# Sparse attention and MLP in one kernel: ScalarE instead of GpSimd scales the words of the weights in the first slots, and the first unit of weights moves ahead in ScalarE's order

## The chip, the cores and the metric

The kernel runs on one core of a Trainium2 chip. A core has five engines with instruction streams of their own, which meet only at semaphores: TensorE (PE; its weight loads are listed as PEld), VectorE (DVE), ScalarE (ACT), GpSimd (POOL) and SyncE (SP), which here issues most of the transfers. The metric is the device time of one execution in microseconds (us), as the median of several runs. Before the change it is 1530.93 us.

## What is computed

The reference is top-k attention followed by an MLP with an exact GELU, all in float32:

```python
scores = scale * np.matmul(q, k.transpose(0, 1, 3, 2))      # 8 x 8 heads, 576 x 576, head_dim 64
kth = np.partition(scores, -32, axis=-1)[..., -32:-31]
scores = np.where(scores >= kth, scores, -1e9)
attn = np.exp(scores - scores.max(-1)) ; attn /= attn.sum(-1) + 1e-9
x = (attn @ v).transpose(0, 2, 1, 3).reshape(4608, 512)
h = x @ w_in                                                 # 512 x 2048
out = (0.5 * h * (1 + erf(h / sqrt(2)))) @ w_out             # 2048 x 512
```

## The kernel before, in words

The program is written with a manual schedule: each engine executes its instructions in the order in which the Python code emits them, and waits in that order.

**Items and slots.** Two heads make a pair, and 128 query rows of both heads of a pair make an item. A loop (`for n in range(ahead)`, L1086) emits one slot for each item. In slot n several items are under way at different stages: the scores of item n+2 (`scores`: PE's L339 for the last keys and L376 for the rest, brought out of PSUM by ACT's L347 and L384), the 32 largest values of item n on DVE (`top_k`: MAX8 in L471, MATCH_REPLACE8 in L474, with lists made by DVE's L412 and POOL's L437 and L445), the mask and exponential of item n-1 on ACT (`select`, L505, twice, and `softmax`, L517, twice, with the row sums `den`), the transposes of item n-2 (PE's L561 and L595 in the first slots, where the factor 1/den is put in by a diagonal matrix; L567 and L597 later; ACT's copies L577 and L602), and the product with v for item n-3 in every second slot (PE's L659, copied into xT by ACT's L664).

**What ties the engines together in a slot.** POOL first adds the unit of weights of this slot (L233), then does `smaller(n+1)` (L445), `add_small(n-1)` on den (L498), `threshold(n)` (L485 neg, L486 bias), `normalise(n-1)` (L531, the tile `diag`) and `sum_up(n+2)` (L437). DVE takes the reciprocal of den of item n-1 (L492) at the end of `top_k(n)`, so DVE waits there for POOL's L498, and that one for ACT's L517. PE's L561 waits for `diag`.

**The opening.** START is 10. In the slots 0 to 9 the MLP has not begun: PE fills up with matmuls on idle data (`keep_busy`, L1045, tile `warm`). The MLP's first matmul (L717, `h_ps`) comes in slot 10, as soon as xT is there. Afterwards pieces of the MLP are strewn over the slots. The pairs 0 to 3 are transposed by PE in the slots up to 3 (L287, tile `tp_qk`, copied by L292 into `kt` and `qm`); these pieces are kept in `prep_in`, and slot 0 has the keys of the third pair.

**The weights.** w_in and w_out come in as 16 units of 128x2x512 words, one for each of the slots 1 to 10 and 13 to 18. They are float64 in memory; a unit comes by two transfers on SP's queue, one for each 128 rows (`load_weights`, L190), into parts of w_out_sb and w_sum that aren't in use yet, and is turned into float32 by four instructions over its words: L207 on ACT (from the high words, into `below`), a scaling of the words `w` by 2**-13 as integers, L218 on ACT (`below` to the destination `d`), and L233 on POOL (d + w). The scaling does not depend on L207. It is done by DVE (L209) in the slots 13 to 18, by POOL (L213) in the slots 3, 5, 7 and 9 (`ON_POOL = range(3, START, 2)`), and by ACT (L217) in the rest. The first three belong to `weights_size`, which is called at the end of slot n for the unit of slot n+1 (L1188); the add stands first in slot n+1 (L1093). `load_weights(n+2)` stands behind it at the end of slot n, and a unit's buffer is the one of the unit two slots earlier, save for some that use w_sum, so its transfers wait for that unit's L233.

Of the kernel before, what the change touches and what calls it, by code (L numbers as in the profile page):

```python
# [14 lines left out]
def kernel(  # L15
# [19 lines left out]
    nc = tc.nc  # L35
    f32, i32, u32 = mybir.dt.float32, mybir.dt.int32, mybir.dt.uint32
    bf16, i16, u16 = mybir.dt.bfloat16, mybir.dt.int16, mybir.dt.uint16
    AF = mybir.ActivationFunctionType
    ALU = mybir.AluOpType
# [108 lines left out]
    START = 2 * NP + 2  # L148
    WARM = 9
    PAIRED = 0  # L150
    ON_DVE = range(START + 1, START + 9)
    ON_POOL = range(3, START, 2)
    DIAGS = START - 1
    SINGLE = range(18, 28)
    words = {}
# [7 lines left out]
    SLOT_OF = dict(zip(ORDER, [*range(1, START + 1), *range(START + 3, START + 9)]))  # L163
    UNIT_IN = {n: u for u, n in SLOT_OF.items()}
    unit_in = UNIT_IN.get
# [30 lines left out]
    def parts(u):  # L196

        t, dst = words[u], weights_of(u)[3].bitcast(i32)
        return t[:, :, 0::2], t.bitcast(mybir.dt.int16)[:, :, 2::4], t[:, :, 1::2], dst

    def weights_size(u):


        if u not in words:
            return
        w, first, below, d = parts(u)
        nc.scalar.activation(below, first, func=AF.Prelu, bias=high, scale=2.0**-40, alpha=2.0**40)  # L207
        if on_dve(u):
            nc.vector.tensor_scalar(  # L209
                w.bitcast(i32), w.bitcast(u32), 2.0**-13, None, op0=ALU.mult  # L210
            )
        elif SLOT_OF[u] in ON_POOL:
            nc.gpsimd.tensor_scalar(  # L213
                w.bitcast(i32), w.bitcast(u32), 2.0**-13, None, op0=ALU.mult
            )
        else:
            nc.scalar.activation(w.bitcast(i32), w.bitcast(u32), func=AF.Copy, scale=2.0**-13)  # L217
        nc.scalar.activation(d, below, func=AF.Prelu, bias=low, scale=2.0**59, alpha=2.0**-40)  # L218

    def on_dve(u):  # L220

        return SLOT_OF[u] in ON_DVE

    def waits(u):

        return u == ORDER[-1]
# [3 lines left out]
    def weights_add(u):  # L230
        if u in words:
            w, _, _, d = parts(u)
            nc.gpsimd.tensor_tensor(d, d, w.bitcast(i32), op=ALU.add)  # L233
        made.add(u)
# [129 lines left out]
    def scores(i, second=False):  # L364
        if i >= N or i in S_of:
            return
        pair, t = items[i]
        S_of[i] = s = work.tile([P, 2 * S], f32, tag="s", bufs=6, name="s")
        s_ps = pair_tile("s_ps", "l1" if second else "pr")
        if not few[0]:  # L370
            last_keys(i, bank("t_ps"))()
        if t < NM:
            q_t, kt = q_of[pair][:, t * P : (t + 1) * P], kt_of[pair]
            for e in range(2):
                rows = slice(e * D, (e + 1) * D)
                nc.tensor.matmul(  # L376
                    s_ps[:, e], lhsT=q_t[rows, :], rhs=kt[rows, 0:SM], start=True, stop=True
                )
            if i == 0:

                nc.scalar.activation(s[:, 0:SM], s_ps[:, 0], func=AF.Copy, scale=scale)
                nc.scalar.activation(s[:, S + TL :], s_ps[:, 1], func=AF.Copy, scale=scale)  # L382
                return
            nc.scalar.activation(spread(s, S + TL, SM), s_ps, func=AF.Copy, scale=scale)  # L384
        else:

            for r in range(2):
                kt = kt_of[pair + r]
                for e in range(2):
                    rows = slice(e * D, (e + 1) * D)  # L390
                    nc.tensor.matmul(  # L391
                        s_ps[half(r, e), r, :], lhsT=kt[rows, SM + P + e * TL : SM + P + (e + 1) * TL],
                        rhs=kt[rows, 0:SM], start=True, stop=True,
                    )
            s2 = s.rearrange("p (r n) -> p r n", r=2)
            nc.scalar.activation(s2[:, :, 0:SM], s_ps, func=AF.Copy, scale=scale)
# [12 lines left out]
    def larger(i):  # L409

        if paired(i):
            nc.vector.tensor_tensor(lists_of[i][:, :, 0], *halves_of(i), op=ALU.max)  # L412
# [87 lines left out]
    def select(i, e):  # L500

        if i < 0 or i >= N:
            return
        st, s = stat_of[i], row(i, e)
        nc.scalar.activation(s, s, func=AF.Prelu, bias=st["neg"][:, e : e + 1], scale=1.0, alpha=STEEP)  # L505
        selected.add((i, e))
# [113 lines left out]
    def closes(i):  # L620

        if not few[0] or i < 0 or i >= N:
            return False
        pair, t = items[i]
        return t < NM and t % 2 == 1 and pair % NP == NP - 1

    def copy_x():
        while copies:
            copies.pop()()
# [393 lines left out]
    def room_in(n):  # L1023

        x = n - START - 1
        if x < 1:
            return 4
        if x >= len(sizes):
            return 0
        return sizes[x] + (1 if x % 2 == 0 else -1)  # L1030
# [55 lines left out]
    for n in range(ahead):  # L1086

        left[0] = room_in(n)
        few[0] = n > START + 2
        eager[0] = n > N  # L1090
        left[0] += closes(n - 3) - closes(n - 2)
        if not waits(unit_in(n)):
            weights_add(unit_in(n))  # L1093
        if n > 0:
            larger(n + 1)
        for piece in squares_in.pop(n, []):
            piece()
        two = few[0] and n % 2 == 0 and n + 3 < N and items[n + 3][1] < NM
        scores(n + 2, two)
        if two:  # L1100
            scores(n + 3)
        product = attend(n - 3)
        late = n > START
        if n < START:

            for e in range(2):
                select(n - 1, e)
            softmax(n - 1, 0)
        copy_x()
        if n == START:  # L1110

            for e in range(2):
                select(n - 1, e)
            softmax(n - 1, 0)
        if waits(unit_in(n)):
            weights_size(unit_in(n))
            weights_add(unit_in(n))
        mlp(1)
        if closes(n - 3):
            ready[0] = n_tok[0]  # L1120
        if few[0] and n % 2:
            run_gelus()
        tr = transposes(n - 2)
        if product and n > START and done[0] < len(pieces) and pieces[done[0]][0] > ready[0]:

            for piece in tr[:1]:
                piece(n + 2 if few[0] else None)
            tr, ready[0] = tr[1:], n_tok[0]
        if not few[0] and n > START:
            softmax(n - 1, 0)  # L1130
        mlp(1)
        if not late:
            softmax(n - 1, 1)
        if few[0]:
            softmax(n - 1, 0)
            if n % 2:
                mlp(ODD)
        mlp(1)
        prep = prep_in.pop(n, [])
        if n == START + 1:  # L1140

            for piece in prep:
                piece(None)
            prep = []
        if len(prep) > 1 and len(tr) == 3:
            tr, prep = tr[:1] + prep[:1] + tr[1:], prep[1:]
        now = tr[:-1]
        if few[0]:
            now, tr, prep = tr + prep[:1], [], prep[1:]
        for x, piece in enumerate(now):  # L1150
            piece(n + 2 if few[0] else None)
            ready[0] = n_tok[0]
            if few[0] and x == 2:
                break
            mlp(1)
        ready[0] = n_tok[0]
        if late:
            softmax(n - 1, 1)
        if n > 0:
            smaller(n + 1)  # L1160
        add_small(n - 1)
        for piece in tr[-1:] + prep:
            piece(None)
            mlp(1)
        if n < START:

            keep_busy(4 if n == 0 else 8 if product else 20 if n == 1 else 14 if n < 5 else 18, ident)

        run_gelus()
        mlp(left[0])  # L1170
        run_gelus()
        if n < N:
            top_k(n, lambda: inverse(n - 1))
            if n == 0:
                larger(1)
        else:
            inverse(n - 1)
        threshold(n)
        if n == 0:
            smaller(1)  # L1180
        normalise(n - 1)
        sum_up(n + 2)
        if n in sums_in:
            weight_sums(sums_in[n])
        run_small(6)

        if not waits(unit_in(n + 1)):
            weights_size(unit_in(n + 1))  # L1188
        for m in (n + 1, n + 2):

            if m > 2 and waits(unit_in(m)) == (m == n + 1):
                load_weights(m)
        if n < NP:
            load("v", n)
        if n == 5:
            load("q", SQUARES)
            load("k", SQUARES)
# [38 lines left out]
```

## Time and profile before

| | |
|---|---|
| median of 3 runs | 1530.93 us (1529.75 to 1532.0) |
| the profiled execution | 1529.7 us, its span 1527.8 us |
| granted clock of TensorE, mean | 0.996 |
| PE busy | 1508.4 us (99%) |
| DVE busy | 1235.3 us (81%) |
| ACT busy | 1152.8 us (75%) |
| POOL busy | 1149.9 us (75%) |
| L213 on POOL | 4 instructions |
| L217 on ACT | 6 instructions |

A timeline row of the profile gives the start in us from the begin of the span, the duration, the engine, the line of the kernel, the operation, the tiles (out<-in), shapes and types and, in brackets, how long the engine was idle before and what ended that. Consecutive instructions of ACT overlap a little, so starts are subtracted from starts where the cost of one in its sequence is asked for. A row of a chain of waits gives the start and the length of the piece, with the engine and line that it is put down to. A row of the waits gives the engine and line that waited, for whom, the us in total, the number of times and the longest. A row of busy time by stretches gives the stretch and its length, then the busy us (with the number of instructions) of PE, PEld, DVE, ACT and POOL, the granted clock, the share of the transfers, and GB/s.

### The profile page before, as it was taken

The numbers are of one execution on the slowest core, as the hardware profiler recorded it, in microseconds if no ns is written. First come the engines' busy times: TensorE is split into PE (matmuls) and PEld (weight loads), VectorE is DVE, ScalarE is ACT, GpSimd is POOL, SyncE is SP. The second block draws the span as 40 slices with busy tenths as digits, with TensorE's granted clock in tenths as the row PEclk, the third lists the DMA queues.
The fourth block names the chain that finished last, engine by engine and source line by source line (L and its number), as shares of the span: only waits on it lengthen the run. The fifth ranks groups of instructions, "written<-read, shape, count | busy, mean of one in ns | idle before, by whom it ended". The sixth has DMA issues, their size and how long they took to land.

```text
span 1527.8 us, 26920 instructions
## 1 busy us (share of the span) xinstructions
PE 1508.4 (99%) x9233; PEld 1191.6 (78%) x9233; DVE 1235.3 (81%) x3270; ACT 1152.8 (75%) x2034; POOL 1149.9 (75%) x1295
## 2 busy tenths in 40 slices
PE   7999999999999999999999999999999999999999
PEld 5776677887777778888877778788787777888887
DVE  7889899988888878788888887888888887877701
ACT  6989977777877787877777777787777878787730
POOL 6997667867887868777797878786788786877742
PEclk9999999999999999999999999999999999999999
DMA  6424310021101110012201111011110111000000
GB/s 178 134 101 116 85 46 1 22 37 34 24 19 28 38 40 15 1 30 47 39 15 22 27 30 46 1 25 36 32 24 22 24 30 32 15 1 15 8 14 14
DMA packets 195016, 56.27 MB, mean 37 GB/s; under 512 B 185888, under 2 KB 186432, under 8 KB 194880
## 3 DMA queue, kind: packets, MB, share of 16 engines
q1 hardware_dynamic: 193616, 54.14, 15.1%
q8 instruction: 72, 1.18, 0.3%
q14 instruction: 64, 0.52, 0.1%
q10 hardware_dynamic: 1200, 0.39, 0.1%
q0 software_dynamic: 64, 0.03, 0.0%
HBM read 45.08 MB, written 9.44 MB: 36 GB/s over the span
## 4 chain that ended last, share of the span: by engine, by line
PE 93%; DVE 3%; POOL 2%; DMA 1%; SPq 0%; ACT 0%; issue 0%; DVEq 0%
PE h_ps L717 34%; PE y_ps L861 20%; PE o L659 9%; PE tp L597 8%; PE s_ps L376 7%; PE seven L859 3%; PE y_ps L823 2%; PE y_ps L805 2%; PE y_ps L826 2%; PE tp_t L339 2%; PE o L670 1%; PE s_ps L391 1%; PE tp_t L567 1%; DVE top L471 1%; DVE lists L474 1%; POOL w_out_sb L213 1%
## 5 line engine op out<-in xcount | busy, mean ns | idle before, releaser
L717 PE MATMUL h_ps<-xT,w_in_sb 128*128 128x256 f32 (+1 forms) x2560 | 544.0, 361 | 0.0
L717 PEld LDWEIGHTS h_ps<-xT,w_in_sb 128*128 128x128 f32 x2560 | 433.8, 191 | 70.8 <-issue 25.3
L471 DVE MAX8 top<-lists 128x8 f32<-128x576 f32 (+1 forms) x792 | 477.2, 642 | 0.1
L474 DVE MATCH_REPLACE8 lists<-top,lists 128x288 f32<-128x288 f32 (+1 forms) x528 | 307.4, 587 | 0.0
L540 POOL TENSOR_TENSOR s<-s,rden 128x1152 f32<-128x1152 f32 x135 | 285.4, 2114 | 0.3 <-DVE rden L492 0.3
L498 POOL TENSOR_SCALAR den<-den 128x2 f32<-128x2 f32 x144 | 31.7, 220 | 280.3 <-ACT s L517 278.4
L517 ACT ACTIVATE s<-s,bias 128x576 f32<-128x576 f32 x288 | 223.3, 776 | 11.6 <-issue 0.7
L505 ACT ACTIVATE s<-s,neg 128x576 f32<-128x576 f32 x288 | 224.6, 784 | 0.0
L611 ACT COPY pt<-tp 128x1024 f32<-128x1024 f32 x133 | 135.1, 1016 | 110.7 <-PE tp L597 110.7
L492 DVE RECIPROCAL rden<-den 128x2 f32<-128x2 f32 x144 | 23.7, 164 | 218.4 <-POOL den L498 218.1
L445 POOL TENSOR_TENSOR lists<-lists 128x576 int32<-128x576 int32 x132 | 186.3, 1412 | 4.0
L437 POOL TENSOR_TENSOR lists<-s 128x576 int32<-128x576 int32 x133 | 187.1, 1407 | 0.0
L659 PE MATMUL o<-pt,raw_v 128*64 128x256 f32 x1280 | 152.9, 384 | 0.7 <-ACT pt L602 0.4
L659 PEld LDWEIGHTS o<-pt,raw_v 128*64 128x64 f32 x1280 | 86.3, 136 | 85.9 <-issue 44.3
L861 PE MATMUL y_ps<-w_out_sb,sum 128*128 128x256 f32 x472 | 140.4, 379 | 0.0
L597 PE MATMUL tp<-ident,s 128*128 128x128 f32 x1080 | 140.1, 273 | 0.0
L597 PEld LDWEIGHTS tp<-ident,s 128*128 128x128 f32 x1080 | 126.4, 141 | 14.5 <-issue 1.9
L384 ACT ACTIVATE s<-s_ps 128x1024 f32<-128x1024 f32 x127 | 124.1, 1024 | 12.0 <-PE s_ps L376 11.6
L376 PE MATMUL s_ps<-kt,qm 64*128 64x512 f32 x512 | 130.3, 622 | 0.8 <-ACT s L382 0.8
L474 DVE MATCH_REPLACE8 lists<-first,lists 128x288 f32<-128x288 f32 x264 | 114.1, 437 | 0.0
L861 PE MATMUL y_ps<-w_out_sb,g 128*128 128x256 f32 x480 | 113.4, 379 | 0.0
L733 ACT ACTIVATE g<-h_ps 128x512 f32<-128x512 f32 x144 | 78.2, 595 | 42.1 <-PE h_ps L717 41.5
(164 smaller groups left out, 2517.2 us busy)
## 6 DMA issues: line engine op xcount, KB each, us to landing
raw_v<-in_v_dram SPq DMA_DIRECT2D x64, 128.0 KB, 2.3
out_dram<-y SPq DMA_DIRECT2D x30, 256.0 KB, 2.0
raw_q<-in_q_dram SPq DMA_DIRECT2D x112, 64.0 KB, 2.0
raw_k<-in_k_dram SPq DMA_DIRECT2D x112, 64.0 KB, 2.0
w_out_sb<-in_moe_w_in_dram SPq DMA_DIRECT2D x14, 511.8 KB, 4.7
w_out_sb<-in_moe_w_out_dram SPq DMA_DIRECT2D x10, 511.8 KB, 4.3
w_sum<-in_moe_w_out_dram SPq DMA_DIRECT2D x6, 511.8 KB, 4.1
raw_q<-in_q_dram SPq DMA_DIRECT2D x112, 8.0 KB, 1.8
```

The costliest lines, as they stand in the source:

```text
L376: nc.tensor.matmul(s_ps[:, e], lhsT=q_t[rows, :], rhs=kt[rows, 0:SM], start=True, stop=True)
L437: nc.gpsimd.tensor_tensor(t[:, :, 1].bitcast(i32), a.bitcast(i32), b.bitcast(i32), op=ALU.add)
L445: nc.gpsimd.tensor_tensor(into_of(i)[:, :, 1].bitcast(i32), both, top, op=ALU.subtract)
L471: nc.vector.max(x[:, e], src[:, e])
L474: nc.vector.match_replace(dst[:, e], x[:, e], src[:, e], LOWEST)
L505: nc.scalar.activation(s, s, func=AF.Prelu, bias=st["neg"][:, e : e + 1], scale=1.0, alpha=STEEP)
L517: nc.scalar.activation(s, s, func=AF.Exp, bias=st["bias"][:, e : e + 1], scale=1.0, accum_out=st["den"][:, e : e + 1],)
L540: nc.gpsimd.tensor_tensor(s, s, wide, op=ALU.mult)
L597: nc.tensor.transpose(to, part, ident)
L659: nc.tensor.matmul(o[e * D : (e + 1) * D, 0:n], lhsT=vt[:, j, e, :], rhs=pt[:, e * NM + j if j < NM else 2 * NM, :], start=(j == 0), stop= ...
L717: nc.tensor.matmul(h_tile(u)[:, i, :], lhsT=w_in_sb[:, ko, f * P : (f + 1) * P], rhs=xT[:, ko, c0 : c0 + n], start=(ko == 0), stop=(ko == ...
L861: nc.tensor.matmul(acc[names][:, k], lhsT=lhsT, rhs=rhs, start=(j == 0 and k == 0), stop=(j == FT // 2 - 1 and k == 1),)
```

## The change

Two edits, both within the opening. First, the branch for POOL goes, so that the units of the slots 3, 5, 7 and 9 are scaled by ACT between L207 and L218, like those of the other slots up to 10. Second, in slot 0 the call of `weights_size` for the unit of slot 1 moves from the slot's end to a point ahead of the pieces in `prep_in`, that is, ahead of the transpose of the third pair's keys and of ACT's copy of them; it issues three instructions on ACT and none elsewhere, and SP's and POOL's orders keep theirs.

```diff
     ON_DVE = range(START + 1, START + 9)
-    ON_POOL = range(3, START, 2)
...
             nc.vector.tensor_scalar(
                 w.bitcast(i32), w.bitcast(u32), 2.0**-13, None, op0=ALU.mult
             )
-        elif SLOT_OF[u] in ON_POOL:
-            nc.gpsimd.tensor_scalar(
-                w.bitcast(i32), w.bitcast(u32), 2.0**-13, None, op0=ALU.mult
-            )
         else:
             nc.scalar.activation(w.bitcast(i32), w.bitcast(u32), func=AF.Copy, scale=2.0**-13)
...
         prep = prep_in.pop(n, [])
+        if n == 0:
+            weights_size(unit_in(1))
         if n == START + 1:
...
-        if not waits(unit_in(n + 1)):
+        if n > 0 and not waits(unit_in(n + 1)):
             weights_size(unit_in(n + 1))
```

## The prediction

> **What bounds the kernel now.** I read the page's chain first, then busy time by stretches from the point where the MLP starts, then the chain of waits inside the first 103 us, then the waits of each engine there, then ACT's rows one by one.
>
> ```profile
> PE 93%; DVE 3%; POOL 2%; DMA 1%; SPq 0%; ACT 0%; issue 0%; DVEq 0%
> ```
>
> ```profile
> 103.20:200.00 96.80, 96.35 (x536) 62.72 (x537) 89.69 (x230) 84.83 (x137) 68.26 (x61) 1.00 0.35 91
> ```
>
> TensorE is 93% of the chain, and from 103.2 us on it is busy for 96.35 of 96.80 us, at full clock. So after the slots 0 to 9 nothing but PE's own work sets the end, and the change, which lies wholly in these slots, can only move the moment at which PE begins its MLP. The other 7% of the chain, 107 us, is this opening. There the chain of waits reads differently:
>
> ```profile
> 39.39 2.99 POOL w_sum L213
> 46.32 0.23 POOL den L498
> ...
> 102.50 0.62 POOL diag L531
> 103.16 0.44 PE tp_t L561 x4
> ```
>
> ```profile
> DVE rden L492 <- POOL den L498: 8.9, 4, 2.2
> ```
>
> ```profile
> 46.57 0.17 DVE L492 RECIPROCAL rden<-den 128x2 f32<-128x2 f32 x1 [2.21 <-POOL den L498]
> 54.59 0.14 DVE L492 RECIPROCAL rden<-den 128x2 f32<-128x2 f32 x1
> 101.65 0.17 DVE L492 RECIPROCAL rden<-den 128x2 f32<-128x2 f32 x1 [2.23 <-POOL den L498]
> ```
>
> In the slots with odd numbers 3, 5, 7, 9 the chain runs through POOL: the scaling of the words (L213, 2.99 us), then the add of the unit, then the small den that DVE waits for. DVE needs 54.59 - 46.57 = 8.02 us for a slot without that wait, and it waits four times, 8.9 us in all. The chain leaves the opening by POOL's diag of slot 9, which starts at 102.50 and ends when PE starts L561 at 103.16. Read so far, the change should bring nearly 9 us. It won't, because PE's first MLP matmul (L717) needs a second thing, the copy of o into xT (L664), and that stands in ACT's order.
>
> **The change part by part: the four Copies.** It removes four L213 from POOL and adds four L217 to ACT, one in each of the slots 2, 4, 6, 8 (for the units of slots 3, 5, 7, 9). ACT issues in order, so the cost of one is read between starts, where the same pair of rows stands with and without it:
>
> ```profile
> 62.43 1.26 ACT L207 ACTIVATE w_out_sb<-w_out_sb,high 128x1024 f32<-128x1024 int16 x1
> 63.58 1.15 ACT L217 ACTIVATE w_out_sb<-w_out_sb 128x1024 int32<-128x1024 uint32 x1
> 64.61 1.28 ACT L218 ACTIVATE w_out_sb<-w_out_sb,low 128x1024 int32<-128x1024 f32 x1
> 65.76 0.30 ACT L347 ACTIVATE s<-t_ps 128x128 f32<-128x128 f32 x1
> 65.91 1.05 ACT L384 ACTIVATE s<-s_ps 128x1024 f32<-128x1024 f32 x1
> 66.82 1.48 ACT L505 ACTIVATE s<-s,neg 128x576 f32<-128x576 f32 x2
> ...
> 70.08 1.13 ACT L602 COPY pt<-tp 128x512 f32<-128x512 f32 x2
> 71.03 1.29 ACT L207 ACTIVATE w_out_sb<-w_out_sb,high 128x1024 f32<-128x1024 int16 x1
> 72.35 1.22 ACT L218 ACTIVATE w_in_sb<-w_out_sb,low 128x1024 int32<-128x1024 f32 x1
> ```
>
> With L217, L207 to L218 takes 64.61 - 62.43 = 2.18 us; without, 72.35 - 71.03 = 1.32. One Copy costs ACT 0.86 us, four cost 3.44. Nothing hides them unless ACT idles now. Where it does:
>
> ```profile
> 40.10 0.25 ACT L347 ACTIVATE s<-t_ps 128x128 f32<-128x128 f32 x1
> 40.97 1.02 ACT L384 ACTIVATE s<-s_ps 128x1024 f32<-128x1024 f32 x1 [0.62 <-PE s_ps L376]
> ...
> 77.52 1.19 ACT L602 COPY pt<-tp 128x512 f32<-128x512 f32 x2
> 79.13 1.27 ACT L207 ACTIVATE w_out_sb<-w_out_sb,high 128x1024 f32<-128x1024 int16 x1 [0.41 <-DMA w_out_sb<-in_moe_w_in_dram]
> ...
> 81.33 1.25 ACT L218 ACTIVATE w_in_sb<-w_out_sb,low 128x1024 int32<-128x1024 f32 x1
> 83.03 0.28 ACT L347 ACTIVATE s<-t_ps 128x128 f32<-128x128 f32 x1 [0.44 <-PE t_ps L339]
> 84.10 1.02 ACT L384 ACTIVATE s<-s_ps 128x1024 f32<-128x1024 f32 x1 [0.79 <-PE s_ps L376]
> ...
> 100.01 0.30 ACT L347 ACTIVATE s<-t_ps 128x128 f32<-128x128 f32 x1
> 100.80 1.02 ACT L384 ACTIVATE s<-s_ps 128x1024 f32<-128x1024 f32 x1 [0.48 <-PE s_ps L376]
> 103.13 0.37 ACT L664 COPY xT<-o 128x256 f32<-128x256 f32 x1 [1.31 <-PE o L659]
> ```
>
> Against the undisturbed steps of the fence before (L347 to L384 0.15, L384 to the next 0.91, L602 to L207 0.95, L218 to L347 1.15) ACT loses 0.72 at 40.97, 0.66 at 79.13, 0.55 at 83.03, 0.92 at 84.10, 0.64 at 100.80 and 1.42 at 103.13: 4.91 us in all. These are waits for PE (and one for a transfer), and PE was late because it waited for POOL's diag. With POOL relieved I take all of them as gone, and in their place stand the four Copies: 3.44 - 4.91 = -1.47 us at L664. **ACT becomes the bound of the slots 2 to 9**, with no idle time left. L384 of slot 10 stays where it is: 100.80 - (4.91 - 1.42) + 3.44 = 100.75; L664 starts 0.91 later, at 101.66 instead of 103.13.
>
> Is anything else late then? DVE's next release comes from ACT's exponentials through POOL's den, as it does already in slot 4:
>
> ```profile
> 49.82 1.06 ACT L384 ACTIVATE s<-s_ps 128x1024 f32<-128x1024 f32 x1
> ```
>
> ```profile
> 54.07 0.22 POOL L498 TENSOR_SCALAR den<-den 128x2 f32<-128x2 f32 x1 [0.40 <-ACT s L517]
> ```
>
> den starts 4.25 us after L384. An even slot has the xT copy in it and an odd one has not, so 4.0 to 4.25, and 0.26 more to the reciprocal (46.57 - 46.32). From there to L384 of slot 6 (65.91) ACT takes 16.09 for two slots without a wait; with the Copy that slot 4 gets, 16.95, or 8.5 a slot, above DVE's floor of 8.02. So L384 of slot 9 stands some 8.4 ahead of 100.75, near 92.3, and its reciprocal comes near 96.7 instead of 101.65, 5 us earlier; diag ends 1.5 us behind it (103.16 - 101.65), at 98.2. PE has diag in hand before L664 starts, and is bound by ACT alone.
>
> POOL keeps the add of each unit, and the add waits for L218, which ends 0.86 later in these slots. But POOL has 2.99 us less to do ahead of it, so den no longer hangs on it except by some tenths in slot 3. The transfers of later units wait for that add on SP's queue; slot by slot it ends no later than now, since the 0.86 is less than the 2.99. The one transfer that ACT waited for (0.41 at 79.13) is freed by an add that ended behind a delayed POOL. I cost POOL and SP at nothing.
>
> **The change part by part: the move.** In slot 0 the three instructions of the first unit go ahead of the kt copy:
>
> ```profile
> 19.87 0.58 ACT L292 COPY kt<-tp_qk 128x512 f32<-128x512 f32 x1 [3.76 <-PE tp_qk L287]
> ...
> 24.02 1.02 ACT L384 ACTIVATE s<-s_ps 128x1024 f32<-128x1024 f32 x1
> ```
>
> ```profile
> 8.91 5.99 DMA w_out_sb<-in_moe_w_in_dram
> 14.92 3.73 DMA raw_k<-in_k_dram
> ```
>
> ```profile
> 21.89 2.08 PE L376 MATMUL s_ps<-kt,qm 64*128 64x512 f32 x4
> ```
>
> ACT idles 3.76 us there, from 16.1 on, and the three take 2.18 + 1.15 = 3.33. The weights that the chain waits for have landed at 14.90 (8.91 + 5.99), so L207 can start near 16.1 and L218 ends by 19.5; the kt copy keeps its 19.87. That frees ACT behind the kt copy for 3.3 us. But L384 at 24.02 starts when PE's s_ps ends (21.89 + 2.08 = 23.97), and PE hangs there on the third pair's keys, which land at 18.65 (14.92 + 3.73), not on ACT. So the move is worth **nothing** on the path; POOL's first add comes earlier, into slack. If L207 found its data late and started after 16.5, the kt copy would slip by as much, and 3 us of slack behind it take that up.
>
> **The sum.** -1.47 us. The profiled execution took 1529.7 us, a span of 1527.8 and 1.9 around it, and lies 1.2 under the median of the runs, 1530.93. So the span goes to 1526.3, an execution like it to 1528.2, and the median to **1529.5**. The bounds of the unknowns: if only the waits that POOL's lateness explains directly go (not the 0.72 of slot 3) the gain is 0.8; the price of a Copy, 0.84 to 0.88 by the starts shown, moves the sum by 0.1. With the scatter of about 1.1 of the runs the forecast's own range is 1528.3 to 1530.7.
>
> **The rivals.**
> 1. *The move counts (faster).* PE's s_ps of slot 1 takes 2.08 us, and ACT hangs on its end; if the same matmuls came at twice that pace, or were released by as much earlier, about 1.0 to 2.1 us would come off all that follows, since ACT is the bound from 24.02 on. With the 1.47 that is 2.5 to 3.6, in the upper case 1527.3. For it: ACT is free for it in the changed order. Against: PE waits there for a transfer, which the change leaves alone. Beside it, a Copy could cost less in company; the four at nothing would give 4.9, 1526.0. Chance 0.18.
> 2. *PE's clock falls at the start of the MLP.* PE would stand idle ahead of L717 for about 1.3 us: L664's wait for o, 1.31 now, turns into PE's wait for L664. In slot 7 a longer wait was followed by slow rows:
>
> ```profile
> 74.70 0.44 PE L561 MATMUL tp_t<-diag,s 128*64 128x128 f32 x4 [2.75 <-POOL diag L531]
> 75.07 3.02 PE L595 MATMUL tp<-diag,s 128*128 128x128 f32 x16
> ...
> 93.03 0.44 PE L561 MATMUL tp_t<-diag,s 128*64 128x128 f32 x4 [1.40 <-POOL diag L531]
> 93.39 2.05 PE L595 MATMUL tp<-diag,s 128*128 128x128 f32 x16
> ```
>
>    Against the rows of slot 9, sixteen L595 took 3.02 instead of 2.05, 0.97 us; as much again for the matmuls behind them makes some 1.7 us. That would give 1531.2, no change. Against: the wait would be 1.3, and the one of 1.40 in slot 9 is followed by the fast rows. The Trainium skill, TensorE: Matmul & The Clock Gate, Part 1, says that the clock is halved after at least one idle window of some 3.4 us; the trace saw it after 2.75, so the page's figure is not taken, and by either 1.3 is short of it. Chance 0.08.
> 3. *ACT pays and PE gives nothing back (slower).* If PE's s_ps and o in the slots 3 to 10 don't come earlier, ACT's waits stay and the Copies add to them: L664 3.44 us later, 1534.4. It decides at PE's diag: if diag of slot 7 and 9 doesn't start at least as much earlier as ACT is later. For it: every engine waits for another in turn here, and ACT's exponentials set den once POOL is free. Against: the 8.9 us of DVE's waits for den, which are POOL's alone in four of four cases. Chance 0.07.
> 4. *The change doesn't do what it says*: the waits only change places, PE's start stays at 103.5, 1530.9. Chance 0.07.
>
> **How the numbers follow.** The forecast has 0.60. The range runs from 1526.0 (the end of rival 1) to 1532.5, past rivals 2 and 4 with the scatter, and leaves out rival 3 and the tails. A measurement of this kernel tells 0.2% from no change, 3.1 us: faster is under 1527.9, slower over 1534.0. Faster: 0.15 of rival 1 and 0.04 from the forecast's lower tail, 0.19. Slower: 0.06 of rival 3 and 0.01, 0.07. The rest, 0.74, is the same.
>
> **What would show it.** ACT's rows: L217 in each slot, no wait of ACT over 0.2 us from 32 to 101, L384 of slot 10 near 100.8, L664 near 101.7, L717 near 102.1. DVE's waits for den smaller than 1 us each, its reciprocal of slot 9 near 96.7, and diag no longer ahead of PE's first MLP matmul in the chain, ACT in its place. In slot 0, L207 near 16.1 and L384 of slot 1 still at 24.0. It is wrong if L384 of slot 1 comes well before 24.0, if ACT still waits for PE in slots 7 to 10, or if PE's rows behind 103 take longer than now.

## The result, and the profile after

The changed kernel takes 1527.05 us (1526.42 to 1527.97), against 1530.93 (1529.75 to 1532.15) before: the ratio is 0.9974, its 95% interval 0.9965 to 0.9984. That is 3.9 us or 0.26% faster. The forecast was 1529.5, in a range of 1526.0 to 1532.5; the direction was right and the gain is 2.6 times the one that was summed. The profiled execution took 1526.42 us, with a span of 1524.5: 3.3 less than the span before.

Lines move up by five in the changed kernel (the first of the weights' lines by one), and by a few more or less in the runs below: L206, L212 and L213 are the weights' three instructions on ACT (L207, L217 and L218 before), L228 POOL's add, L379 the copy of the scores, L597 the copy of the transposes, L654 o, L659 the copy of o into xT, L556 the first transposes with diag, L712 the MLP's first layer, L487 the reciprocal, L493 den, L1040 the fill matmuls. The chain on the page of the changed kernel, by engine:

```profile
PE 93%; ACT 0%; DVE 0%; issue 0%; POOL 0%; DVEq 0%
```

These shares add up to 93%, because the chain now goes back only to 83.97 us. It cannot say what bounded the opening before that. From there it runs over ACT's scores and exponentials of slot 8, POOL's den and diag, and then PE's own row of slot 9 without a wait:

```profile
84.14 0.92 ACT s L379
...
89.36 0.62 POOL diag L526
...
100.30 1.06 PE h_ps L712 x4
```

DVE's waits between 24 and 102 us, before and then in the changed kernel, and two of its reciprocals in the changed kernel's timeline:

```profile
DVE rden L492 <- POOL den L498: 10.8, 5, 2.2
```

```profile
DVE rden L487 <- POOL den L493: 5.5, 8, 1.6
```

```profile
88.50 0.17 DVE L487 RECIPROCAL rden<-den 128x2 f32<-128x2 f32 x1 [0.59 <-POOL den L493]
96.86 0.17 DVE L487 RECIPROCAL rden<-den 128x2 f32<-128x2 f32 x1 [0.26 <-POOL den L493]
```

In the slots 3, 5, 7 and 9 DVE waited 2.2 us each time; the fifth wait, in slot 1, was 1.96. Now it waits in eight of nine slots, 1.59 us in slot 1, 1.04 in slot 4 and less in the others, and the reciprocal of slot 9 comes at 96.86 instead of 101.65. ACT's rows, in slots 0 and 1 and then in slots 9 and 10:

```profile
16.34 1.21 ACT L206 ACTIVATE w_out_sb<-w_out_sb,high 128x1024 f32<-128x1024 int16 x1
...
19.83 0.59 ACT L287 COPY kt<-tp_qk 128x512 f32<-128x512 f32 x1
...
23.99 1.02 ACT L379 ACTIVATE s<-s_ps 128x1024 f32<-128x1024 f32 x1 [1.74 <-PE s_ps L371]
```

```profile
96.31 1.34 ACT L597 COPY pt<-tp 128x512 f32<-128x512 f32 x2
...
100.81 1.28 ACT L379 ACTIVATE s<-s_ps 128x1024 f32<-128x1024 f32 x1
101.71 0.64 ACT L659 COPY xT<-o 128x256 f32<-128x256 f32 x1
```

No row of ACT between 30 and 102 us has a wait in brackets any more. L379 of slot 10 stands at 100.81, where it was at 100.80. But PE did not stay behind the copy at 101.71:

```profile
90.02 0.44 PE L556 MATMUL tp_t<-diag,s 128*64 128x128 f32 x4 [1.02 <-POOL diag L526]
90.39 2.05 PE L590 MATMUL tp<-diag,s 128*128 128x128 f32 x16
92.28 4.18 PE L1040 MATMUL warm<-ident 128*128 128x128 f32 x36
...
97.68 2.40 PE L654 MATMUL o<-pt,raw_v 128*64 128x256 f32 x20
99.89 0.41 PE L556 MATMUL tp_t<-diag,s 128*64 128x128 f32 x4
100.23 1.13 PE L712 MATMUL h_ps<-xT,w_in_sb 128*128 128x256 f32 x4
...
102.08 1.03 PE L712 MATMUL h_ps<-xT,w_in_sb 128*128 128x256 f32 x4
```

The MLP begins at 100.23 instead of 103.53, 3.3 earlier, and that is the whole difference of the spans. It begins 1.5 us before the copy that the prediction made it wait for.

### The profile page after: what moved, and what is told of

Read it like the earlier page. It is cut to its first block, busy times and chain, and to the rows that moved or that the text cites. A ratio compares the mean times of both kernels' runs of the same rounds, so it can differ in the third digit from the quotient of the medians.

```text
span 1524.5 us, 26920 instructions
## 1 busy us (share of the span) xinstructions
PE 1507.2 (99%) x9233; PEld 1191.5 (78%) x9233; DVE 1235.8 (81%) x3270; ACT 1156.2 (76%) x2038; POOL 1137.7 (75%) x1291
## 4 chain that ended last, share of the span: by engine, by line
PE 93%; ACT 0%; DVE 0%; issue 0%; POOL 0%; DVEq 0%
PE h_ps L712 34%; PE y_ps L856 20%; PE o L654 9%; PE tp L592 8%; PE s_ps L371 7%; PE seven L854 3%; PE y_ps L818 2%; PE y_ps L800 2%; PE y_ps L821 2%; PE tp_t L334 2%; PE o L665 1%; PE s_ps L386 1%; PE tp_t L562 1%; PE tp_t L348 0%; PE warm L1040 0%; PE tp L590 0%
## 5 line engine op out<-in xcount | busy, mean ns | idle before, releaser
L712 PE MATMUL h_ps<-xT,w_in_sb 128*128 128x256 f32 (+1 forms) x2560 | 544.0, 361 | 0.1
L712 PEld LDWEIGHTS h_ps<-xT,w_in_sb 128*128 128x128 f32 x2560 | 433.7, 191 | 71.0 <-issue 25.2
L493 POOL TENSOR_SCALAR den<-den 128x2 f32<-128x2 f32 x144 | 31.6, 219 | 284.5 <-ACT s L512 282.8
L487 DVE RECIPROCAL rden<-den 128x2 f32<-128x2 f32 x144 | 23.8, 165 | 213.8 <-POOL den L493 213.3
L654 PEld LDWEIGHTS o<-pt,raw_v 128*64 128x64 f32 x1280 | 87.1, 136 | 85.2 <-issue 44.3
L654 PE MATMUL o<-pt,raw_v 128*64 128x256 f32 x1280 | 153.0, 384 | 0.7 <-ACT pt L597 0.4
L379 ACT ACTIVATE s<-s_ps 128x1024 f32<-128x1024 f32 x127 | 125.2, 1032 | 11.3 <-PE s_ps L371 11.2
```

Of the source, the lines that this page charges most:

```text
L654: nc.tensor.matmul(o[e * D : (e + 1) * D, 0:n], lhsT=vt[:, j, e, :], rhs=pt[:, e * NM + j if j < NM else 2 * NM, :], start=(j == 0), stop= ...
L712: nc.tensor.matmul(h_tile(u)[:, i, :], lhsT=w_in_sb[:, ko, f * P : (f + 1) * P], rhs=xT[:, ko, c0 : c0 + n], start=(ko == 0), stop=(ko == ...
```

## The experiments

The theory after the result (A): the first edit does all of it; ACT is the bound of the slots 2 to 9; the MLP's start hangs on ACT's copies of slot 9 and on diag, not on the copy of slot 10. The rivals: the move brought the rest (B), PE's own matmuls are the bound now (C), the first MLP matmul does need the copy of slot 10 (D). Each kernel was compared with the kernel before on the same chip; before lay at 1530.6 to 1530.8 in all of them.

### The two edits apart

The first edit without the move:

```diff
-        if n == 0:
-            weights_size(unit_in(1))
...
-        if n > 0 and not waits(unit_in(n + 1)):
+        if not waits(unit_in(n + 1)):
```

> The first edit alone: ACT scales all the words, the first unit stays at the end of slot 0. Theory A (the first edit does all; the MLP's start hangs on ACT's exponentials of slot 8 by way of diag and PE's slot 9, and no longer on POOL; the move falls into a wait of ACT for PE): the time of the changed kernel, 1527.0 us, 3.3 to 3.9 under before, with the scores of slot 1 leaving PSUM at 24.0 as in both kernels. Rival B (the move brings what the recorded sum missed, about 2.4 us, and the Copies the 1.5 that it forecast): 1529.5, 1.5 under before.

Measured: 1527.56, ratio 0.9976 (0.9967 to 0.9985). In its profile the MLP starts at 101.43, 1.2 later than in the changed kernel's, because the scores of slot 3 are late by as much (the reason is below, under the half-clocked stretches).

The move without the first edit, POOL still scaling four units (shown against the changed kernel):

```diff
+    ON_POOL = range(3, START, 2)
...
+        elif SLOT_OF[u] in ON_POOL:
+            nc.gpsimd.tensor_scalar(
+                w.bitcast(i32), w.bitcast(u32), 2.0**-13, None, op0=ALU.mult
+            )
```

> The move alone: POOL still scales the units of slots 3, 5, 7 and 9. Theory A: no change, 1530.9, DVE still waits 8.9 us for den in the odd slots and the MLP starts at 103.5. Rival B (the move is worth about 2.4 us): 1528.5.

Measured: 1530.11, ratio 0.9999 (0.999 to 1.0008). The waits of this kernel between 30 and 100 us:

```profile
DVE rden L492 <- POOL den L498: 7.7, 4, 2.4
```

The waits for POOL are still there: 2.44, 2.03 and 2.22 us in the slots 3, 5 and 7, and 2.19 in slot 9, just behind this stretch; the fourth one counted here is 1.00 in slot 4. The MLP starts at 105.23 in this profile, not at the expected 103.5, since PE's clock was halved in slot 9 (the rows stand in the last section). Rival B falls: the Copies give the gain, and the move alone gives nothing that can be measured.

### Where ACT's time counts

A Copy made a second time, by a factor of 1, once at the end of slot 4 and once, in another kernel, at the end of slot 9 (with 10 in place of 5 in the test of the slot):

```diff
             nc.scalar.activation(w.bitcast(i32), w.bitcast(u32), func=AF.Copy, scale=2.0**-13)
+            if SLOT_OF[u] == 5:
+                nc.scalar.activation(w.bitcast(i32), w.bitcast(i32), func=AF.Copy, scale=1.0)
```

> The changed kernel with the Copy of the unit of slot 5 made twice, the second time by a factor of 1, so that ACT has one more Copy at the end of slot 4, about 1.04 us from start to start. Theory A (ACT is the bound of slots 2 to 8 with no idle time): every later row of ACT is 1.0 later and the MLP's start with it, 101.3 instead of 100.2; 1528.1, 2.8 under before. Rival C (PE's own matmuls or DVE's 8.02 us a slot are the bound now): less than 0.5 us, 1527.1 to 1527.5.

Measured: 1527.9, ratio 0.9982 (0.9974 to 0.9991). ACT's rows at the end of slot 4 and PE's start of the MLP in this kernel:

```profile
56.23 1.28 ACT L212 ACTIVATE w_out_sb<-w_out_sb 128x1024 int32<-128x1024 uint32 x1
57.54 1.16 ACT L214 ACTIVATE w_out_sb<-w_out_sb 128x1024 int32<-128x1024 int32 x1
```

```profile
101.45 1.13 PE L714 MATMUL h_ps<-xT,w_in_sb 128*128 128x256 f32 x4
```

The second Copy costs 57.54 - 56.23 = 1.31: its row starts only where that of the first, whose result it reads, has ended. The MLP starts 101.45 - 100.23 = 1.22 later, of which 0.11 stands already at the scores of slot 3 (41.20 against 41.09). What ACT is given in slot 4 arrives at the MLP's start but for 0.2 us. Rival C falls for this slot.

> The changed kernel with the Copy of the unit of slot 10 made twice, at the end of slot 9, behind that slot's copies of the transposes; the copy of o into xT in slot 10 is 1.04 us later, 102.75 instead of 101.7. Theory A (the MLP's first piece reads only the first two pairs' columns of xT, which earlier slots wrote): the first MLP matmul stays at 100.2, and only the second piece, at 102.1 in the changed kernel, may wait some 0.5 us for its last matmuls: 1527.0 to 1527.7. Rival D (the step of the record: the first MLP matmul needs the copy of slot 10): the start is 1.0 later, 1528.1.

Measured: 1528.16, ratio 0.9985 (0.9977 to 0.9994). This lies outside A's range, and by its time alone it is D's number, so the trace has to decide. ACT's scores of slot 3 came at 42.04 in this profile, 0.95 later than in the changed kernel's (the reason is below), and all that follows carries that. ACT's copy, and PE's rows:

```profile
42.04 1.02 ACT L381 ACTIVATE s<-s_ps 128x1024 f32<-128x1024 f32 x1 [0.79 <-PE s_ps L373]
...
103.97 0.38 ACT L661 COPY xT<-o 128x256 f32<-128x256 f32 x1
```

```profile
101.04 1.13 PE L714 MATMUL h_ps<-xT,w_in_sb 128*128 128x256 f32 x4
...
102.90 0.60 PE L714 MATMUL h_ps<-xT,w_in_sb 128*128 128x256 f32 x2
104.40 0.70 PE L714 MATMUL h_ps<-xT,w_in_sb 128*128 128x256 f32 x2 [0.90 <-ACT xT L661]
```

The first piece of the MLP starts at 101.04, which is 100.09 without the 0.95, as early as in the changed kernel, and 2.9 before the copy. It contracts over the first two pairs' columns of xT, which earlier slots wrote. The second half of the second piece is what needs the copy, 0.90 us of wait. D falls as it was put, and is right one piece later: a further 1.3 us of ACT in slot 9 costs PE 0.9 there, so in the changed kernel the copy had some 0.4 us to spare.

### What the Copies cost, and what bounds beside them

The scaling of the four units left out, and POOL's add of these units made with a tile of zeros (the units lack their low words, so part of the weights' precision is left out):

```diff
-        else:
+        elif SLOT_OF[u] not in (3, 5, 7, 9):
             nc.scalar.activation(w.bitcast(i32), w.bitcast(u32), func=AF.Copy, scale=2.0**-13)
...
-            nc.gpsimd.tensor_tensor(d, d, w.bitcast(i32), op=ALU.add)
+            if SLOT_OF[u] in (3, 5, 7, 9):
+                z = pt_end.bitcast(i32)
...
+                nc.gpsimd.tensor_tensor(d4, d4, z, op=ALU.add)
+            else:
+                nc.gpsimd.tensor_tensor(d, d, w.bitcast(i32), op=ALU.add)
```

> The changed kernel with the scaling of the units of slots 3, 5, 7 and 9 left out, and POOL's add of these four units made with a tile of zeros instead of their words, so that its cost stays: no engine scales. It shows what the four Copies cost where they stand now. Theory A: ACT loses 0.86 us four times, but DVE's 8.02 us a slot then bounds the slots behind slot 4; the reciprocal of slot 8 comes at 86.5 instead of 88.5, and the MLP starts 2.0 earlier, at 98.2: 1525.0, 5.9 under before. Rival (the Copies cost their full 3.44): 1523.6. Rival (they cost nothing where they stand, PE is the bound): 1527.0.

Measured: 1525.81, ratio 0.9965 (0.9952 to 0.9979), 1.2 to 1.8 under the changed kernel by the medians of that one and of the first edit alone. In the profile, slot 3 is late as in the one of the first edit alone, so these two are compared: first the scores of slot 3 and the MLP's start of the first edit alone, then the scores of slot 3, DVE's reciprocal of slot 8 and the MLP's start without scaling:

```profile
42.32 1.02 ACT L379 ACTIVATE s<-s_ps 128x1024 f32<-128x1024 f32 x1 [0.79 <-PE s_ps L371]
```

```profile
101.43 1.13 PE L712 MATMUL h_ps<-xT,w_in_sb 128*128 128x256 f32 x4
```

```profile
41.78 1.02 ACT L385 ACTIVATE s<-s_ps 128x1024 f32<-128x1024 f32 x1 [0.79 <-PE s_ps L377]
```

```profile
87.35 0.17 DVE L493 RECIPROCAL rden<-den 128x2 f32<-128x2 f32 x1
```

```profile
99.20 1.13 PE L718 MATMUL h_ps<-xT,w_in_sb 128*128 128x256 f32 x4
```

The MLP starts 2.2 us earlier, but 0.5 of that stands already at the scores of slot 3: the first edit alone lacks the move, and its scores of slot 1 come at 23.85 against 23.20 here. From slot 3 on it is 1.7, for three Copies that take 2.58; the one of slot 2 lies ahead of a row of ACT that waits for PE in both. So the Copies cost neither 3.44 nor nothing. Without them DVE's reciprocal has no wait in its row from slot 5 on, and DVE is the next bound, as A expected: its reciprocals of slots 4 to 9 (55.10 to 95.34) come 8.05 us apart.

The four units scaled by DVE:

```diff
-    ON_DVE = range(START + 1, START + 9)
+    ON_DVE = [3, 5, 7, 9, *range(START + 1, START + 9)]
```

> The changed kernel with DVE instead of ACT scaling the four units (0.69 us each in the trace of before). Theory A: ACT is relieved of 3.44, DVE needs 8.71 in four of the slots and 8.02 in the others, and is the bound then: the reciprocal of slot 8 near 87.8 instead of 88.5, the MLP's start 0.7 earlier; 1526.3, 4.6 under before. Rival (DVE was the hidden floor all along, its four times 0.69 come on top): 1529.8.

Measured: 1526.93, ratio 0.9973 (0.9963 to 0.9982). The expected 0.7 against the changed kernel does not show in the time. In the profile, with a late slot 3, the MLP starts at 100.89, 0.5 before that of the first edit alone, and all of that stands already at the scores of slot 3 (41.84 against 42.32). DVE does get ahead: from the reciprocal of slot 3 to that of slot 8 it takes 42.40 us (46.05 to 88.45), against 43.20 (46.52 to 89.72) in the first edit alone. POOL's neg then gives it back:

```profile
88.62 1.32 POOL L480 TENSOR_SCALAR neg<-top 128x2 f32<-128x2 f32 x1 [1.11 <-DVE rden L487]
```

It took 0.22 in the first edit alone. So diag of slot 8 starts 1.60 behind the reciprocal (90.05) and not 0.85 (90.57). DVE's scaling runs beside this row, from 88.52 on; that it is the cause was not tried, and spans on POOL are rough. Nothing speaks for the rival's 1529.8.

Less fill of PE at the end of slot 9:

```diff
-            keep_busy(4 if n == 0 else 8 if product else 20 if n == 1 else 14 if n < 5 else 18, ident)
+            keep_busy(4 if n == 0 else 8 if product else 20 if n == 1 else 14 if n < 5 else 8 if n == 9 else 18, ident)
```

> The changed kernel with 16 instead of 36 fill matmuls of PE at the end of slot 9, 2.2 us less. Theory A: PE then waits for ACT's copies of the transposes of slot 9, which end at 97.6, just where the product with v starts now: no change, 1527.0. Rival C (PE's own row of matmuls in slot 9 is the bound): the MLP starts 0.5 to 1.6 earlier, 1525.5 to 1526.5.

Measured: 1526.68, ratio 0.9973 (0.9963 to 0.9984), no change. PE's rows of slot 10:

```profile
97.54 2.64 PE L654 MATMUL o<-pt,raw_v 128*64 128x256 f32 x19 [1.70 <-ACT pt L597]
...
100.55 1.13 PE L712 MATMUL h_ps<-xT,w_in_sb 128*128 128x256 f32 x4
```

The start at 100.55 carries 0.36 from the scores of slot 1 (24.35 against 23.99), so it has not moved. PE comes early and waits 1.70 for ACT's copies. That is the wait that the chain of the changed kernel hides: there PE's row and ACT's copies end within 0.1 us of each other, and the chain names PE. Rival C falls for slot 9 too, as far as PE alone is meant: the two end together there.

Both of the last edits together:

> Both of the last two edits together, the scaling on DVE and 16 instead of 36 fill matmuls in slot 9. Theory A: ACT's copies of slot 9 end near 95 then, PE arrives early, and diag of slot 9, near 98.0, sets the start of the MLP: 98.4, 1.9 earlier than in the changed kernel; 1525.2, 5.7 under before. Rival C (the fill matmuls are the bound in both): 2.2 less than with the scaling on DVE alone. Rival (neither edit matters): 1527.0.

Measured: 1525.11, ratio 0.9963 (0.995 to 0.9975). PE's rows:

```profile
98.60 0.44 PE L556 MATMUL tp_t<-diag,s 128*64 128x128 f32 x4 [0.25 <-POOL diag L526]
98.97 1.13 PE L712 MATMUL h_ps<-xT,w_in_sb 128*128 128x256 f32 x4
```

With ACT relieved the fill is on the path, and without the fill diag is, as expected. Each edit alone can hardly be told from the changed kernel; together they bring 1.9 by the medians.

### The half-clocked stretches

In both kernels PE waits for the third pair's keys in slot 0, 3.71 us before and 3.34 after, and then runs at a granted clock of 0.50 (from 19 to 24 us). More fill matmuls in that wait:

```diff
         prep = prep_in.pop(n, [])
+        if n == 0:
+            keep_busy(13, ident)
```

> The changed kernel with 13 more fill matmuls of PE (some 3.0 us) in slot 0, in the wait for the third pair's keys, so that PE's clock is not halved when they land. Theory A (the move was worth nothing because PE, at half clock, brought the scores of slot 1 later than ACT could take them): they leave PSUM near 21.8 instead of 24.0, DVE's reciprocal of slot 1 comes near 26.7 instead of 28.2, and the MLP starts 1.5 to 2.2 earlier: 1524.9 to 1525.6. Rival (the keys' landing alone sets slot 1, the clock doesn't matter): 1527.0.

Measured: 1525.49, ratio 0.9965 (0.9953 to 0.9977).

> The same fill without the move: the first unit's three instructions stand behind the kt copy again. Theory A: now ACT is late in slot 1, its scores leave PSUM at 23.7 to 23.9 whatever PE's clock, and the gain of the fill is gone but for 0.1 to 0.3: 1526.7 to 1527.0; so the move is worth 1.3 to 2.0 beside a PE at full clock. Rival (the move is worth nothing in any case): the time of the run with the fill and the move.

Measured: 1527.09, ratio 0.9976 (0.9966 to 0.9985). The scores of slot 1 with the move:

```profile
21.90 1.02 ACT L379 ACTIVATE s<-s_ps 128x1024 f32<-128x1024 f32 x1 [0.79 <-PE s_ps L371]
```

and without it, then PE's wait ahead of its next scores:

```profile
23.36 1.03 ACT L379 ACTIVATE s<-s_ps 128x1024 f32<-128x1024 f32 x1
```

```profile
28.02 0.49 PE L334 MATMUL t_ps<-kt,qm 128*128 128x128 f32 x2 [1.21 <-ACT qm L287]
```

The granted clock is 1.00 from 19 to 26 us in both. With PE at full clock ACT waits for PE when the unit has moved (0.79), and PE for ACT when it has not (1.21). The MLP starts at 99.45 and at 100.96: the move is worth 1.5 us in these profiles and 1.6 by the medians. The 99.45 is only 0.8 before the changed kernel's start, where 1.5 to 2.2 was expected, since the clock was halved in slot 2 of this profile.

Beside a half-clocked PE the move brings nothing to the end, but not because nothing moves. In the profile of the move alone the scores of slot 1 come at 23.31 instead of 24.02; then PE's wait in slot 2 is longer, 2.75 instead of 2.42, the clock is halved behind it, and the scores of slot 3 come at 41.89 instead of 40.97.

The Trainium skill says (TensorE: Matmul & The Clock Gate, Part 1) that the clock is released again by some 3.4 us of activity, counted in a window that runs freely, so that the moment differs from run to run. The trace agrees in that the moment differs: from 22 to 24 us the granted clock is 0.50 in the changed kernel's profile and 0.95 in that of the run that follows here, whose instructions are the same up to slot 2.

The same in slot 2, in PE's wait for ACT's copies:

```diff
-        for piece in tr[-1:] + prep:
+        for x, piece in enumerate(tr[-1:] + prep):
+            if n == 2 and x == 1:
+                keep_busy(9, ident)
             piece(None)
```

> The changed kernel with 9 more fill matmuls (2.1 us) in slot 2, in PE's wait for ACT's copies ahead of the third and fourth pairs' transposes. In some profiles of this study PE's clock is halved after that wait (granted 0.50 from 36 to 38 us) and slot 3's scores leave PSUM at 41.8 to 42.3, in others, that of the changed kernel among them, the clock stays and it is 41.1. Theory A: the fill keeps the clock in every execution, and the median falls by a part of the 1.0: 1526.2 to 1527.0. Rival (the fill itself delays the transposes and the slot): 1527.5 to 1528.

Measured: 1526.3, ratio 0.9971 (0.996 to 0.9983), inside the expected range and hardly to be told from the changed kernel. What it removes is seen in PE's rows of slot 2, of the changed kernel first, then of the first edit alone, then with the fill:

```profile
36.05 0.44 PE L282 MATMUL tp_qk<-ident,w_sum 128*128 128x128 f32 x2 [2.39 <-ACT pt L572]
36.33 3.29 PE L1040 MATMUL warm<-ident 128*128 128x128 f32 x28
```

```profile
35.88 0.69 PE L282 MATMUL tp_qk<-ident,w_sum 128*128 128x128 f32 x2 [2.74 <-ACT pt L572]
36.36 4.63 PE L1040 MATMUL warm<-ident 128*128 128x128 f32 x28
```

```profile
35.31 0.44 PE L282 MATMUL tp_qk<-ident,w_sum 128*128 128x128 f32 x2 [0.73 <-ACT pt L572]
35.59 3.29 PE L1040 MATMUL warm<-ident 128*128 128x128 f32 x28
```

A wait of 2.74 is followed by the slow rows (4.63 for 28 matmuls instead of 3.29, at a granted clock of 0.50 from 36 to 38 us), and that is the late slot 3 of several profiles here.

All four together (DVE, less fill in slot 9, more in slots 0 and 2):

> The fastest so far (the scaling on DVE, 16 instead of 36 fill matmuls in slot 9) with both fills, in slots 0 and 2. Theory A: slot 1 about 1.5 earlier and slot 3 without the halved clock; DVE at 8.0 to 8.7 a slot is the bound then: 1523.0 to 1524.0, some 7.5 under before. Rival (what the fills bring is lost to DVE's row, which is the bound already): 1525.1.

Measured: 1522.03, ratio 0.9944 (0.9931 to 0.9956), one microsecond under what was expected. It beats both kernels, by 8.6 us and by about 5. DVE's reciprocal of slot 9 and PE's start of the MLP:

```profile
93.92 0.15 DVE L487 RECIPROCAL rden<-den 128x2 f32<-128x2 f32 x1
```

```profile
95.65 0.44 PE L556 MATMUL tp_t<-diag,s 128*64 128x128 f32 x4 [0.25 <-POOL diag L526]
96.02 1.13 PE L712 MATMUL h_ps<-xT,w_in_sb 128*128 128x256 f32 x4
```

DVE and the diag behind it set the start, 7.5 us earlier than in the kernel before.

## Why the prediction was right or wrong

- **That only the moment counts at which PE begins the MLP: right.** The start moved by 3.3, the span by 3.3.
- **The price of a Copy, and ACT as the new bound: right.** L379 of slot 10 was put at 100.75 and came at 100.81, the xT copy at 101.66 and 101.71, the reciprocal of slot 9 at 96.7 and 96.86. ACT has no wait left, and the Copy made twice in slot 4 delays the MLP by nearly what it costs. That the rows fit to 0.2 us is luck in part: the walk had no term for PE's clock in slot 2, and in the profile of the first edit alone, where it was halved, L379 of slot 10 came at 102.03. POOL and the transfers took no part, as costed: no row of ACT waits for a transfer any more.
- **The step that failed: "PE's first MLP matmul (L717) needs a second thing, the copy of o into xT (L664)".** The first piece of the MLP reads the first two pairs' columns of xT, which were there long before (so "as soon as xT is there", in the description of the opening, does not hold for the copy of slot 10), and is held by its place in PE's order alone: behind o and behind the transposes with diag. The copy of slot 10 is needed by the second half of the second piece, 2.3 us later (102.08 and half its 1.03, against 100.23). So the sum had to be made at o: ACT's copies of slot 9 end at 97.65, o starts at 97.68 and takes 2.2, L556 0.34, and the MLP starts at 100.23. All but o's length was in the walk; -3.3 was to be had from it in place of -1.47. Nor is PE "bound by ACT alone": its own row from 90.02 on, fill included, ends at the same moment, as the two runs with less fill show. The statement that the copy "turns into PE's wait for L664" fell with it.
- **The move at nothing: right in the number, not in the reason.** The prediction had PE hang on the landing of the keys. In the run with the fill in slot 0 PE began the keys' transposes no earlier (19.05 against 18.71), and the scores of slot 1 still came 2.1 us earlier (21.90 against 23.99): the half clock had hidden the move, and 1.6 us stood behind it. Rival 1 had nearly the measured time (1527.3) and the right place for the move, PE's scores of slot 1, but it did not cause this gain: the first edit gives it without the move.
- **Rival 2** did not occur: the waits ahead of the MLP are short, since PE does not wait for the copy. **Rivals 3 and 4** fell by the rows: ACT's waits are gone, and PE's start moved.
- **The chances** put 0.74 on no change by more than 0.2%, and the gain was 0.26%. The sum's own range, 1528.3 to 1530.7, misses the measured 1527.05; the stated one holds it only because it was stretched to the end of rival 1, which did not occur. That is luck. The check that would have found the error was open before: in the kernel before, L717 starts at 103.53 and the copy at 103.13, close enough to look like its cause; but which columns a piece contracts over stands in the code (`l1_piece`, the range of ko).

## What to carry to other kernels

When the busiest engine waits for two things, look up in the code which of its instructions reads which, before the sum is made at one of them: here a matmul followed a copy by 0.03 us after its end and did not depend on it. When work moves from a late engine to another, walk the receiving engine's order row by row from start to start; here that gave the two rows that were forecast, seven slots ahead, within 0.1 us, in a profile in which PE's clock stayed up in slot 2. And try small edits together where two engines end within 0.1 us of each other: alone each brings nothing, since the other holds the place.

## What was not expected of the hardware

A wait of PE of 2.39, 2.41, 2.42 or 2.65 us in slot 2 left its clock at full speed in the profiles; one of 2.62, 2.74 or 2.75 there halved it, for 3 us or so. The length of the wait alone does not decide. In the profile of the move alone two waits of the same length stand in slots 7 and 9, the first followed by fast rows (granted clock 1.00), the second by slow ones (0.50 from 94 to 96 us):

```profile
75.06 0.44 PE L561 MATMUL tp_t<-diag,s 128*64 128x128 f32 x4 [2.74 <-POOL diag L531]
75.43 2.05 PE L595 MATMUL tp<-diag,s 128*128 128x128 f32 x16
...
93.42 0.44 PE L561 MATMUL tp_t<-diag,s 128*64 128x128 f32 x4 [2.74 <-POOL diag L531]
93.79 3.68 PE L595 MATMUL tp<-diag,s 128*128 128x128 f32 x16
```

The Trainium skill (TensorE: Matmul & The Clock Gate, Part 1) speaks of an idle window of some 3.4 us; here 2.62 sufficed once, so the measurement differs from it. What decides between two equal waits is not shown.

The clock may make much of the scatter of the kernel. The 5 runs of the last experiment, in which both waits are filled, lie within 0.2 us (1521.99 to 1522.18), those of the kernel before within 2.4. But with slot 0 alone filled the runs lie within 2.5, with slot 2 alone within 0.9, and with the scaling on DVE and less fill in slot 9, no wait filled, within 0.6; so the filled waits are not shown to be the whole cause.

Records of ACT get longer while ACT doesn't idle, though its pace doesn't change. Two rows of the changed kernel, of the same instruction, each 0.15 or 0.16 ahead of the next one's start:

```profile
31.83 0.27 ACT L342 ACTIVATE s<-t_ps 128x128 f32<-128x128 f32 x1
...
100.65 0.52 ACT L342 ACTIVATE s<-t_ps 128x128 f32<-128x128 f32 x1
```

In such a stretch the cost of an instruction is read from start to start, not from its duration.
